# Attention scores in three steps of 512 columns, and an instruction order planned with a fuller model of TensorE

## Chip, cores, metric

One NeuronCore of one Trainium2 chip. The metric is the device time of one execution in microseconds (us), median over several executions. An execution is called *slow* when it is more than 1.5% above the fastest of the same kernel; ratios use the other, *fast*, executions alone. The 95% interval of a ratio is given in brackets.

## The reference, cut

Causal attention with a decay (8 batches, 8 heads, 576 positions, 64 columns a head), then a mixture of experts that sends each whole batch to one of 8 experts.

```python
def _attn_ref(q, k, v, f):                    # q, k, v: 8 x 8 x 576 x 64
    scores = scale * q @ k^T
    cum = np.cumsum(np.log(np.clip(f, 0.0001, 1.0)), axis=-1)
    scores = where(causal, -1e9, scores + cum[:, :, :, None] - cum[:, :, None, :])
    attn = softmax(scores)
    return attn @ v
def _moe_ref(x, w_gate, w1, w2):              # x: 8 x 576 x 512, w1: 8 x 512 x 1024, w2: 8 x 1024 x 512
    logits = x.mean(axis=1) @ w_gate          # one row a batch
    e = argmax(logits); gate = softmax(logits)[e]
    out = gate * (np.maximum(x @ w1[e], 0) @ w2[e])
```

## The kernel before

A *quad* is four heads of one batch, so there are 16. The kernel does not fix the order of its instructions by hand. It lists operations with a duration, an engine, what they wait for and which buffers they take. A small planner (class `Order`) then plays the schedule forward on the host and emits each instruction when its model of the chip would start it. The planner's times are a model; only the order reaches the chip. Each engine works its queue in order, so an instruction that waits holds up all behind it.

```python
STEPS = (((0, 0, 448, 0),),                       # (key chunk, first query, last query, column)
         ((1, 128, 576, 0),),
         ((2, 256, 576, 0), (4, 512, 576, 320)),
         ((3, 384, 576, 0), (0, 448, 576, 192)))
WIDTH = (448, 448, 384, 320)
FILL = 60.0
PM0 = 12.0
LAG = 3
...
    HOP = 0.12                                     # from one engine's end to another's start
...
            if best is None and self.filler is not None and now < self.fill_until and busy["PE"] <= now + 1e-9:
                ...self.filler(ok[0][1])           # a matmul on a zero tile, to keep TensorE busy
...
    def gate6(op, b):                              # the gate's value to all 128 partitions
        i = od.slot(("gate", b))
        nc.sync.dma_start(GATE[i], ROW[i])
...
        g6 = od.add(f"g6{b}", "SP", .5, lambda op, b=b: gate6(op, b), prio=-5, after=[g5], lands=.2, grain=.02, runs=8)
...
                raws[g, 1].behind = ... [wvs[g - LAG][0]]       # q and k of quad g, loaded behind V of quad g - LAG
...
                hm = od.add(f"H{b}{j}{half}", "PE", .49, ..., after=[ld if b else quarters[j // 2], g6], ...)
```

Note the last line: in the plan the first expert matmuls wait for `g6`. On the chip they do not use the gate; only the ReLU after them does.

The softmax here doesn't subtract the row's maximum and nothing guards it: scores larger than these inputs give would overflow.

## Time and profile before

| | before |
|---|---|
| time, median (lowest to highest) | 252.76 us (252.37 to 253.58), 3 runs |
| profiled span | 250.8 us |
| TensorE / ScalarE / GpSimd / VectorE busy | 92 / 71 / 51 / 46% |
| first gate matmul, first expert matmul | 32.5 us, 39.3 us |
| expert matmuls of the last batch, first kind: first start, last start | 228.4 us, 236.1 us |

The page's lines for the engines, the 40 slices and the chain are in the prediction below. One group is the transfer that spreads the gate. This is the view of all instructions that use the gate's tile in the kernel before: name of the group, durations of the issue, start times; the last line is for its transfers.

```profile
L567 SPq DMA_DIRECT2D gate_b<-row x8: 523/538/567, 35.5 to 216.6; - x8
...
DMA to landing us min/median/max: 2.0/6.3/17.7
```

512 bytes take up to 17.7 us to land; much else is in flight then.

### The profile page before, as it was taken

How to read it: one execution, taken by the hardware profiler on the slowest of the kernel's cores; microseconds unless marked ns; L12 is line 12 of the kernel's file. 1: busy time of each engine (PE TensorE's matmuls, PEld its weight loads, DVE VectorE, ACT ScalarE, POOL GpSimd, SP SyncE). 2: the span in 40 equal slices, each digit the busy share in tenths (PEclk: the TensorE clock that was granted, in tenths of full speed). 3: DMA queues.
4: the chain of work that ended last, by engine and by line, in shares of the span. 5: the costliest groups of instructions: out<-in, count | busy, mean ns of one | idle time of the engine just before them, and what ended most of it. 6: DMA issues, size and time to landing. Idle time of an engine off the chain costs nothing.

```text
span 250.8 us, 8039 instructions
## 1 busy us (share of the span) xinstructions
PE 229.7 (92%) x3304; PEld 146.2 (58%) x3325; DVE 115.4 (46%) x305; ACT 177.2 (71%) x313; POOL 127.0 (51%) x197
## 2 busy tenths in 40 slices
PE   6799997999889999799999999899998999999990
PEld 2333734674366846567458755586586656957840
DVE  3892882667533941278136942694146342200000
ACT  3466846897799968849779874896488787855820
POOL 6046739971995546714992649363822872300000
PEclk9657999999999999979999999999999999999996
DMA  6996849999999999990999999999993598299032
GB/s 119 221 221 118 146 73 180 201 207 212 177 220 212 215 204 226 297 213 8 173 219 213 277 218 215 254 227 209 227 278 76 82 232 216 36 212 256 29 121 75
DMA packets 59946, 45.84 MB, mean 183 GB/s; under 512 B 40896, under 2 KB 43968, under 8 KB 59904
## 3 DMA queue, kind: packets, MB, share of 16 engines
q0 software_dynamic: 14848, 26.22, 59.1%
q1 hardware_dynamic: 32576, 15.90, 25.1%
q10 hardware_dynamic: 12480, 3.15, 6.1%
q8 instruction: 28, 0.46, 0.7%
q14 instruction: 14, 0.11, 0.1%
HBM read 62.03 MB, written 9.44 MB: 285 GB/s over the span
## 4 chain that ended last, share of the span: by engine, by line
PE 73%; DMA 7%; issue 6%; POOL 6%; ACT 3%; DVE 2%; POOLq 1%; ACTq 0%; DVEq 0%
PE ps_w L595 24%; PE ps_w L612 20%; PE ps_s L400 12%; PE ps_w L439 11%; PE ps_w L615 3%; PE ps_w L680 3%; DMA out_dram<-otile 3%; DMA w1e<-in_moe_w_dram 2%; ACT e L406 2%; DMA rawq<-in_q_dram 2%; POOL e L410 2%; POOL vb L423 1%; DVE qt L387 1%; POOL rawk L281 1%; PE ps_w L548 1%
## 5 line engine op out<-in xcount | busy, mean ns | idle before, releaser
L406 ACT ACTIVATE e<-ps_s 128x896 bf16<-128x896 f32 (+2 forms) x128 | 100.2, 834 | 28.7 <-PE ps_s L400 27.9
L410 POOL TENSOR_SCALAR_AFFINE_SELECT e<-e 128x512 bf16<-128x512 bf16 x64 | 41.7, 656 | 69.0 <-ACT e L406 68.4
L595 PE MATMUL ps_w<-xT,w1e 128*128 128x288 bf16 x512 | 71.0, 292 | 3.4 <-DVE xT L459 1.9
L595 PEld LDWEIGHTS <-w1e 128*128 128x128 bf16 x512 | 60.5, 139 | 11.5 <-issue 4.9
L612 PE MATMUL ps_w<-w2e,h1T 128*128 128x512 bf16 x239 | 57.5, 380 | 1.9 <-issue 1.4
L400 PE MATMUL ps_s<-qt,kt 32*128 32x448 bf16 (+4 forms) x768 | 42.1, 289 | 5.6 <-ACT e L406 2.8
L459 DVE SCALAR_TENSOR_TENSOR xT<-ps_w,lr 128x256 bf16<-128x256 f32 (+1 forms) x64 | 26.8, 455 | 37.1 <-ACT lr L449 30.6
L605 ACT ACTIVATE h1T<-ps_w,gate_b 128x288 bf16<-128x288 f32 x77 | 37.4, 499 | 4.9 <-PE ps_w L595 4.7
L612 PEld LDWEIGHTS <-h1T 128*128 128x128 bf16 x256 | 22.8, 98 | 28.5 <-issue 3.6
L603 DVE TENSOR_SCALAR h1T<-ps_w,gate_b 128x288 bf16<-128x288 f32 x51 | 25.3, 505 | 28.6 <-PE ps_w L595 28.2
L400 PEld LDWEIGHTS <-kt 32*128 32x128 bf16 x768 | 17.6, 95 | 27.5 <-issue 21.5
L439 PE MATMUL ps_w<-e,vb 128*32 128x320 bf16 (+4 forms) x1024 | 29.4, 251 | 1.8 <-issue 1.5
L423 POOL TENSOR_TENSOR vb<-vf,WF 128x512 bf16<-128x512 f32 x29 | 30.5, 1053 | 0.3
L387 DVE STREAM_TRANSPOSE kt<-rawk 128x576 f32<-128x576 f32 (+1 forms) x17 | 21.3, 1252 | 19.4 <-DMA rawk<-in_k_dram 16.3
L624 ACT COPY otile<-ps_w 128x512 f32<-128x512 f32 (+1 forms) x25 | 14.0, 560 | 21.9 <-PE ps_w L612 20.9
L439 PEld LDWEIGHTS <-vb 128*32 128x32 bf16 x1024 | 21.3, 97 | 7.0 <-issue 4.7
L387 DVE STREAM_TRANSPOSE qt<-rawq 128x576 f32<-128x576 f32 (+1 forms) x17 | 21.1, 1244 | 0.6 <-DMA rawq<-in_q_dram 0.5
L680 PE MATMUL ps_w<-still 128*128 128x512 bf16 x51 | 17.4, 472 | 2.1 <-DVE still L313 1.4
L622 DVE COPY otile<-ps_w 128x512 f32<-128x512 f32 (+1 forms) x15 | 9.0, 599 | 21.2 <-PE ps_w L612 19.8
L439 PE MATMUL ps_w<-e,WB 128*32 128x192 bf16 (+4 forms) x512 | 17.3, 253 | 0.1
L576 POOL DMA_DIRECT2D w1e<-in_moe_w_dram x14 | 10.2, 731 | 13.1 <-DVE h1T L603 11.4
L444 ACT ACTIVATE lr<-ps_w 128x256 f32<-128x256 f32 (+1 forms) x31 | 12.7, 411 | 4.8 <-PE ps_w L439 4.5
(55 smaller groups left out, 129.4 us busy)
## 6 DMA issues: line engine op xcount, KB each, us to landing
w2e<-in_moe_w_dram POOLq DMA_DIRECT2D x8, 1024.0 KB, 14.2
out_dram<-otile SPq DMA_DIRECT2D x32, 256.0 KB, 7.4
w1e<-in_moe_w_dram POOLq DMA_DIRECT2D x14, 512.0 KB, 7.6
rawk<-in_k_dram POOLq DMA_DIRECT2D x15, 288.0 KB, 7.2
rawq<-in_q_dram POOLq DMA_DIRECT2D x15, 288.0 KB, 8.7
vf<-in_v_dram SPq DMA_DIRECT2D x12, 256.0 KB, 9.3
vf<-in_v_dram ACTq DMA_DIRECT2D x12, 256.0 KB, 12.2
vf<-in_v_dram SPq DMA_DIRECT2D x22, 128.0 KB, 6.0
```

The costliest lines, as they stand in the source:

```text
L387: nc.vector.transpose(dst, raw)
L400: nc.tensor.matmul(ps[:, col:col + i1 - i0], kt[32 * h:32 * h + 32, KLO[c]:KLO[c] + P, r], qt[32 * h:32 * h + 32, i0:i1, r], start=(r == 0 ...
L406: nc.scalar.activation(e[:, 2 * n:2 * n + 2, :], PS_S[od.slot(("s", (g, s, n)))][:, :, 0:WIDTH[s]], AF.Exp, scale=0.125)
L410: nc.gpsimd.affine_select(out=e[:, :, 0:128], in_=e[:, :, 0:128], pattern=[[0, 4], [1, 128]], channel_multiplier=-1, base=0, compare_op=AL ...
L423: eng.tensor_tensor(vb[:, c, :, :], vf[:, c, h, :], WF[:, b, c, h].unsqueeze(3).to_broadcast([P, 2, 4, D]), op=ALU.mult)
L439: nc.tensor.matmul(ps[32 * h:32 * h + 32, lo - i0:hi - i0], lhs, e[s][:, h, col:col + hi - lo], start=(n == 0), stop=(n == len(parts) - 1) ...
L459: nc.vector.scalar_tensor_tensor(XT[od.slot(("x", b))][:, mm, i0:i1], ps[:, 0:i1 - i0], 1.0 if (g, blk) in ON_DVE else LN_SCALE, LR[od.slo ...
L595: nc.tensor.matmul(ps[:, 0:288], lhs, xT[:, m, 288 * half:288 * half + 288], start=(m == 0), stop=(m == 3))
L603: nc.vector.tensor_scalar(dst, ps[:, 0:288], g[:, 0:1], 0.0, op0=ALU.mult, op1=ALU.max)
L605: nc.scalar.activation(dst, ps[:, 0:288], AF.Relu, scale=g[:, 0:1])
L612: nc.tensor.matmul(ps, h[:, j, P * sb:P * sb + P], r, start=(j == 0), stop=(j == 7))
L680: od.filler = lambda i: nc.tensor.matmul(PS_W[i], still[:, 0:P], still[:, 0:512])
```

## The change

The intent: 3 exponentials of 1024 columns a pair of heads instead of 4 narrower ones; a faster start (fillers only from 28 us, V after the small `f`); and a plan closer to the chip (cold clock, TensorE's instruction blocks of 128 matmuls, corrected durations). With it: GpSimd weights 64 more rows of V, VectorE takes part of the masks and key copies, and the gate is spread by a matmul.

```diff
-STEPS = (((0, 0, 448, 0),), ((1, 128, 576, 0),), ((2, 256, 576, 0), (4, 512, 576, 320)), ((3, 384, 576, 0), (0, 448, 576, 192)))
+STEPS = (((0, 64, 576, 0),),
+         ((1, 128, 576, 0), (None, 0, 64, 448)),
+         ((2, 256, 576, 0), (3, 384, 576, 320)))
+COLD = (1.9, 24.0)
+AHEAD = 34
+FETCH = 5.7
+STALL = 2.0
+MASKS = (2, 3)
-FILL = 60.0
+FILL = (28.0, 60.0)
-PM0 = 12.0
-LAG = 3
+PM0 = 10.0
+LAG = 2
-LOOK = {1: (0, 0, 0), 2: (0, 1, 2), 3: (1, 0, 2), 4: (1, 0, 2)}
+LOOK = {1: (0, 0, 0), 2: (0, 1, 2), 3: (1, 0, 2)}
 ... (planner)
+            if e == "PE" and now < COLD[1]:
+                op.us *= COLD[0]
+            if e == "PE":
+                wait, reached, at = self.stall(op, now)      # the fetch of the next block
+                op.us += wait
 ... (V loads)
-    last = [loadf]
+    last = []
+    mark0 = od.add("mark0", "DVE", .08, lambda op: mark(op, 0), prio=-1, after=[loadf])
 ... (gate)
-        g6 = od.add(f"g6{b}", "SP", .5, ..., lands=.2, grain=.02, runs=8)
+        g6 = od.add(f"g6{b}", "PE", .15, ..., mm=2, prio=-5, after=[g5], takes=(("bank", ("spread", b)),))
+        g7 = od.add(f"g7{b}", "DVE", .1, ...)
-                hm = ... after=[ld if b else quarters[j // 2], g6]
+                hm = ... after=[ld if b else quarters[j // 2]]
 ... (durations of some twelve kinds of operation corrected; clamping of the weights folded into the scan)
```

## The prediction

> **What bounds the kernel now.** I read the page first, then the busy time in 10 us and 1 us windows, the chain in order of time, the groups by form, and the timeline where the windows showed a hole. The page says TensorE for most of the span, and half speed near the start.
>
> ```profile
> PE 229.7 (92%) x3304; PEld 146.2 (58%) x3325; DVE 115.4 (46%) x305; ACT 177.2 (71%) x313; POOL 127.0 (51%) x197
> ...
> PE   6799997999889999799999999899998999999990
> ...
> PEclk9657999999999999979999999999999999999996
> ...
> PE 73%; DMA 7%; issue 6%; POOL 6%; ACT 3%; DVE 2%; POOLq 1%; ACTq 0%; DVEq 0%
> ```
>
> 92% busy does not mean 92% useful: matmul spans overlap, fillers on a zero tile (L680, 17.4 us) count, and at half clock everything counts double. So I counted what the matmuls are worth when the clock is full and nothing is waited for, from the stretches of the chain where one kind follows another directly:
>
> ```profile
> 130.02 0.51 PE ps_s L400 x8
> ...
> 138.62 0.40 PE ps_s L400 x16
> ...
> 228.59 7.84 PE ps_w L595 x64
> 236.43 0.99 PE ps_w L615 x16
> ...
> 237.58 6.87 PE ps_w L612 x31
> ```
>
> Per batch the first expert matmuls cost 7.84 us, the second 6.87 + 0.99. A quad (four heads; 16 of them) takes 0.51 + 0.51 + 0.45 + 0.40 = 1.87 for scores, and, from 0.61, 0.70 and 1.16 pieces of L439 in the same view, 2.47 for attention times values. Gate matmuls: about 0.28 a batch. Sum: 8 x 7.86 + 8 x 7.84 + 16 x 4.34 + 2.2 = **197 us of useful TensorE work** out of 250.8. The other 54 us lie in three places.
>
> **(a) Before 44.0 us**, when expert matmuls begin to run without holes. Up to there only 144 of 768 score, 192 of 1536 value and 20 of 512 expert matmuls ran: 3 x 1.87 + 2 x 2.47 + 2.5 = 13 us of work, **31 us lost**. The other loss here is the clock: 1 us windows show it at half from 7.8 to 21.3 us, though TensorE is called busy.
>
> ```profile
> 9.00:10.00 1.00, 1.00 (x5) 0.13 (x2) 0.97 (x2) 0.99 (x2) 0.00 (x0) 0.50 1.20 218
> ...
> 20.00:21.00 1.00, 1.00 (x7) 0.16 (x9) 0.00 (x0) 0.00 (x0) 0.94 (x4) 0.50 0.07 19
> 21.00:22.00 1.00, 1.00 (x28) 0.39 (x28) 0.00 (x0) 0.26 (x1) 0.94 (x3) 0.78 0.34 25
> ```
>
> What fills it is fillers, and they stand ahead of real work in an in-order queue:
>
> ```profile
> 12.73 1.46 PE L680 MATMUL ps_w<-still 128*128 128x512 bf16 x3
> ...
> 18.64 2.31 PE L680 MATMUL ps_w<-still 128*128 128x512 bf16 x5
> ...
> 20.88 0.82 PE L400 MATMUL ps_s<-qt,kt 32*128 32x448 bf16 x8
> ```
>
> The planner expected those scores at another time than the chip delivered them. The path then is: attention of batch 0 done, gate matmul at 32.55, expert index 33.95, weight issues on POOL from 35.5, first expert matmul 39.1, steady at 43.9.
>
> **(b) From 44 to 244.5 us**: 200.5 us holding 184 of work, **16.5 us lost**. Named holes: 67.6 to 74, where scores wait for the exponentials while POOL alone carries the chain (1.0 + 0.44 + 0.26, then 0.43 at 79); 104.5 to 110, where a transpose waiting for its load holds up the normalisations that free a PSUM bank (1.86 idle, then 12 expert matmuls in 3.00 instead of 1.47 us, because the clock fell to half again); instruction fetches in the middle of small matmuls at 159.9 and 188.8 (0.61 and 0.90). Together some 7 us; the rest are array changes and crumbs.
>
> **(c) The end**: 6.3 us from the last matmul to the landed output. From 212.6 us on there is no attention left and TensorE runs without holes, so whatever is saved earlier reaches the end.
>
> **What the Trainium skill says.** "TensorE: Matmul & The Clock Gate", Part 1, has the array at half clock until it was busy for a window of some 3.4 us, and again after an idle one. This trace agrees on the half and on the fall near 106 us, but not on the budget: 13.5 us passed here with TensorE called busy and the clock at 0.50. The same page, "Back-to-back issue gap", gives about N/2.4 + 2.5 ns: 216 ns at 512 and 122.5 at 288 columns; this trace has 216 and 122 to 123 start to start, so columns, not instruction counts, set the price. Part 3 of the page says that matmuls on different row groups run side by side; here four start within 3 to 4 ns, and a group of four costs columns/2.4 plus roughly 12 ns. "SBUF — State Buffer", on its shared port pair, says a VectorE operation with two SBUF inputs and a GpSimd one that reads SBUF shut each other out. The trace fits: weighting V on VectorE took 0.69 us alone at 13.4 us, and 1.23 each at 17.1 us beside GpSimd.
>
> **The change part by part.**
>
> *Scores.* 448/448/384/320 become 3 x 512, and the matmul count stays 48 a quad (8, 24, 16). Steps 0 and 2: 2 x (213 + 12) + 90 ns for the change of array = 0.54, and 2 x (133 + 12) + 2 x (80 + 12) + 90 = 0.56. Step 1 has 2 x (187 + 12) = 0.40 plus 16 of 64 columns whose pairs sit on one row group; the trace has such a pair 29 ns apart, so 8 pairs at about 32 = 0.26, plus 0.09: 0.75. Sum 1.85 against 1.87: **nothing, -0.3 us** over 16 quads. The saved step is eaten by the unshared 64-column pairs.
>
> *Exponentials.* Pairs took 1.73, 1.73, 1.51 and 1.30: 6.27 a quad. Slope from 913 ns at 896 and 807 at 768: 0.83 ns an element; a pair of 1024 is 1.73 + 2 x 0.107 = 1.94, times 3 = 5.83. ScalarE saves 0.44 a quad, 7 us in all, but it is idle 29%; only the first two quads have it on the path (about 0.9 us, inside the start below).
>
> *Values.* Parts go from 2 + 6 to 3 + 5, columns unchanged: 0. *Masks, copies:* POOL sheds 0.4 to 1.3 us a quad when VectorE takes two of five masks, and takes on 0.6 for another 64 rows of V and maybe 0.3 for the copied keys: about even outside quads 2 and 3.
>
> *Gate.* The spreading DMA (6.3 us median to landing, waited for nowhere in this trace) becomes a matmul and a copy: 8 x 0.15 = **+1.2 us** of TensorE, no gain seen.
>
> *Start.* No fillers before 28 us in the plan, half-speed matmuls assumed until 24, V loads held until F has landed, clamping of the weights folded into the scan and the flag postponed. Delays that go: fillers ahead of the transposes of the cumulative sum, 1.0 (scan over 9.45, transposes 10.61); ahead of the second half's first scores 1.0 (bank free near 13.1, issue 14.12); 0.8 at 15.9 to 16.7; 1.4 of the five before 20.88 (last exponential over at 19.44); 0.5 from earlier q and k. Against it, the clock may rise at 24 rather than 21.3 us: half of 2.7 us, some +0.7 to 1.4. Net **-4.0 us**, carried one for one through the gate and the weights.
>
> *Plan.* Fetches cost two holes of 1.5 us; the planner now sees them: -1.2. Masks on VectorE and corrected durations: -1.5 of the 2.1 us at 67 to 79. The bank wait with its cold clock: half of 3.4, -1.7, since nothing in the change aims at it, only truer durations. Sum **-4.4**.
>
> Total -0.3 + 1.2 - 4.0 - 4.4 = -7.5; 252.76 - 7.5 = 245.3, rounded to **245.0 us**.
>
> **Rivals.** *One: the start does not move.* Without fillers the array stays at half speed to 28 us or later, and score and value work there (some 16 us when cold) becomes the bound in place of fillers. For it: half clock lasted 13.5 us even with them. Against it: real work was waiting on fillers, not on TensorE. Then about 249. *Two: holes only move.* DMA is 91% busy by queue shares (59.1 + 25.1 + 6.1), loads of q and k queue behind 2 MB of weights, and a transpose waiting for one blocks VectorE in order, as at 105 us; masks on VectorE lengthen that queue and fight GpSimd for the port. A tighter plan meets this more often. Then -4 at the start and nothing after: 248 to 249. *Three: everything fits.* The truer model removes most of 16.5 us in (b), and batch 0 comes 6 us earlier: 239 to 240.
>
> **Range and chances.** Three parts add: -2 to -6 from the start, 0 to -8 from the plan, +0 to +2 from score pairs and gate. Their likely ends give 240.5 to 249.5. Two per cent faster is 247.7 us, 2.7 above my value with a spread of some 3.5 either way: 0.76 faster, 0.22 within, 0.02 slower (only if the cold start bites and the pairs cost twice my figure).
>
> **What would show it.** Right: the first gate matmul near 28.5 rather than 32.55 us and the first expert matmul near 35; no L680 line before some 25 us; TensorE start to start per quad still near 1.85 for scores; ScalarE's exponentials near 93 us in sum; no TensorE hole over 0.5 us by instruction fetch. Wrong: the clock at 0.50 beyond 26 us; step 1 of the scores over 0.9 us; new idle of TensorE behind VectorE or behind loads of q and k in 60 to 110 us; a chain that runs through the extra V weighting on POOL.

## The result and the profile after

The changed kernel took 256.62 us median (255.8 to 257.48, 4 runs), the kernel before in the same rounds 253.13 (252.37 to 253.58). The ratio is 1.0141, 95% interval 1.0097 to 1.0186: **slower by 1.4%**, within the 2% class, and outside the predicted range of 240.5 to 249.5. All ratios here are the mean time of one kernel's fast runs over that of the kernel before in the same rounds, so not quite the ratio of the medians. On another occasion the same changed kernel came to 1.0307 (1.0216 to 1.0399); the sign is safe, the size is not better known than 1 to 4%. The outputs are right.

The page of the changed kernel, the lines that answer to those in the prediction:

```profile
PE 222.2 (87%) x3284; PEld 145.6 (57%) x3305; DVE 147.7 (58%) x382; ACT 165.1 (65%) x264; POOL 119.3 (47%) x193
...
PE   0838989879999987799998999999999999999990
...
PEclk9999999999999999999999999999999999999998
...
PE 69%; DMA 10%; issue 5%; POOL 5%; DVE 4%; ACT 3%; POOLq 1%; ACTq 0%; DVEq 0%
```

TensorE is busy 7.5 us less, since 34 of its 51 fillers are gone (17.4 us of them before, 4.5 after); VectorE has 32 us more. The chain holds more DMA and VectorE and less TensorE than before. The 15th to 17th slice of TensorE (8, 7, 7; about 89 to 108 us) are the new thin stretch.

Nothing was won at the start: the first gate matmul is at 32.5 us in both, the first expert matmul at 38.9 against 39.3. TensorE's waits in the first 26 us of the changed kernel (what waited, for what: us in total, times, longest):

```profile
PE ps_s L481 <- DVE mid L418: 7.5, 1, 7.5
PE ps_s L481 <- DVE qt L458: 4.1, 1, 4.1
```

The scores of quad 1 wait 4.1 us for its transposed q. GpSimd issued its load only at 10.1 us, after a wait of 2.7 us for V, and the load landed at 17.3; V was itself held until `f` had landed.

TensorE's waits from 44 to 240 us, first before, then after:

```profile
PE ps_s L400 <- ACT e L406: 2.5, 5, 1.0
PE ps_w L595 <- DVE xT L459: 1.9, 1, 1.9
PE ps_w L439 <- issue: 1.5, 2, 0.9
PE ps_w L612 <- issue: 1.4, 9, 0.2
PE ps_w L595 <- DMA w1e<-in_moe_w_dram: 0.5, 1, 0.5
```

```profile
PE ps_s L481 <- ACT e L486: 1.8, 4, 0.6
PE ps_w L712 <- DVE xT L542: 1.7, 1, 1.7
PE ps_w L522 <- POOL e L382: 1.6, 2, 1.0
PE ps_w L729 <- issue: 1.4, 9, 0.2
PE ps_w L522 <- DVE xT L542: 1.4, 1, 1.4
PE ps_w L712 <- DVE h1T L720: 1.2, 2, 0.6
PE ps_w L712 <- ACT lr L527: 1.1, 1, 1.1
PE ps_w L657 <- DVE row L653: 0.5, 1, 0.5
```

The 1.5 us line of L439, which waits for nothing that the profile shows and which I read as instruction fetches, is gone, as intended. In their place stand waits for VectorE, ScalarE and GpSimd. I also counted, from the start times of single matmuls between 44 us and the last expert matmul of the first kind, where the next start came over 0.3 us later than the matmul's own columns explain (0.5 us at a change of kind): **8 holes of 8.0 us before, 14 holes of 12.4 us after**. So there are 4.4 us more of holes, against 3.5 us more of time. A recount by the same rule gave 8.8 us (13 holes) and 12.6 us (16): the small holes near the limit move the count, but hardly the difference. By stretches, most of it lies between 75 and 110 us: there TensorE is idle for 5.1 us (35 less 29.90 busy), before for 2.5 (35 less 32.48).

Two of these holes in the chain of waits of the changed kernel, in order of time (start, us, what); first the one near 54 us, where VectorE stands in order behind a load of k, with the normalisation that TensorE needs queued behind the transpose:

```profile
41.16 12.04 DMA rawk<-in_k_dram
...
53.23 0.04 DVE kt L458
...
54.33 0.50 DVE xT L542 x2
```

and the one from 96 to 106.6 us, where GpSimd alone carries the chain, with masks and weighting of V:

```profile
99.00 1.26 POOL e L382 x2
...
100.33 0.62 POOL vb L510
...
101.02 1.04 POOL vb L506
```

So the trace names suspects: the late loads, the added side work on VectorE and GpSimd (L510 is the added weighting of 64 rows), and the order. The experiments take them one at a time.

### The profile page after: what moved, and what is told of

It is laid out like the page before. It is cut to its first block, busy times and chain, and to the rows that moved or that the text cites.

```text
span 254.8 us, 7985 instructions
## 1 busy us (share of the span) xinstructions
PE 222.2 (87%) x3284; PEld 145.6 (57%) x3305; DVE 147.7 (58%) x382; ACT 165.1 (65%) x264; POOL 119.3 (47%) x193
## 4 chain that ended last, share of the span: by engine, by line
PE 69%; DMA 10%; issue 5%; POOL 5%; DVE 4%; ACT 3%; POOLq 1%; ACTq 0%; DVEq 0%
PE ps_w L712 24%; PE ps_w L729 22%; PE ps_w L522 10%; PE ps_s L481 9%; DMA rawk<-in_k_dram 5%; PE ps_w L732 3%; DMA rawq<-in_q_dram 3%; DMA vf<-in_v_dram 2%; ACT e L486 2%; DVE xT L542 1%; POOL w1e L682 1%; PE ps_w L638 1%; POOL e L382 1%; DVE lr L536 1%; POOL vb L506 1%
## 5 line engine op out<-in xcount | busy, mean ns | idle before, releaser
L486 ACT ACTIVATE e<-ps_s 128x1024 bf16<-128x1024 f32 x96 | 93.2, 1020 | 27.8 <-PE ps_s L481 22.5
L712 PEld LDWEIGHTS <-w1e 128*128 128x128 bf16 x512 | 59.8, 139 | 12.7 <-issue 7.9
L382 POOL TENSOR_SCALAR_AFFINE_SELECT e<-e 128x512 bf16<-128x512 bf16 (+2 forms) x51 | 30.0, 596 | 52.6 <-ACT e L486 52.1
L481 PE MATMUL ps_s<-qt,kt 32*128 32x512 bf16 (+3 forms) x512 | 38.7, 348 | 14.8 <-DVE mid L418 7.5
L720 DVE TENSOR_SCALAR h1T<-ps_w,gate_b 128x288 bf16<-128x288 f32 x71 | 35.7, 515 | 26.2 <-PE ps_w L712 25.2
L722 ACT ACTIVATE h1T<-ps_w,gate_b 128x288 bf16<-128x288 f32 x57 | 28.2, 499 | 18.6 <-PE ps_w L712 17.6
L542 DVE SCALAR_TENSOR_TENSOR xT<-ps_w,lr 128x256 bf16<-128x256 f32 (+1 forms) x64 | 26.6, 453 | 21.2 <-ACT lr L532 18.5
L522 PE MATMUL ps_w<-e,vb 128*32 128x320 bf16 (+3 forms) x1024 | 29.7, 259 | 1.9 <-DVE xT L542 1.4
L481 PEld LDWEIGHTS <-kt 32*128 32x128 bf16 x512 | 12.4, 96 | 30.1 <-issue 15.3
L458 DVE STREAM_TRANSPOSE kt<-rawk 128x576 f32<-128x576 f32 (+1 forms) x17 | 21.3, 1253 | 10.2 <-DMA rawk<-in_k_dram 10.1
L492 DVE TENSOR_TENSOR e<-e,causal 128x512 bf16<-128x512 bf16 (+1 forms) x32 | 17.3, 547 | 9.5 <-ACT e L486 9.4
L668 POOL DMA_DIRECT2D w1e<-in_moe_w_dram x14 | 10.1, 727 | 23.3 <-DVE row L653 11.9
L522 PE MATMUL ps_w<-e,WB 128*32 128x320 bf16 (+3 forms) x512 | 18.5, 264 | 1.8 <-POOL e L382 1.6
L522 PEld LDWEIGHTS <-WB 128*32 128x32 bf16 x512 | 11.8, 99 | 12.5 <-issue 9.8
## 6 DMA issues: line engine op xcount, KB each, us to landing
rawq<-in_q_dram POOLq DMA_DIRECT2D x15, 288.0 KB, 12.6
```

The source lines that it names most:

```text
L382: nc.gpsimd.affine_select(out=x, in_=x, pattern=[[0, x.shape[1]], [1, x.shape[2]]], channel_multiplier=-1, base=base, compare_op=ALU.is_ge ...
L458: nc.vector.transpose(dst, raw)
L481: nc.tensor.matmul(ps[:, col:col + i1 - i0], kt[row, KLO[c]:KLO[c] + P, r], qt[row, i0:i1, r], start=(r == 0), stop=(r == 1))
L486: nc.scalar.activation(e[:, lo:lo + 2, :], banks, AF.Exp, scale=0.125)
L492: nc.vector.tensor_tensor(x, x, keep.unsqueeze(1).to_broadcast([P, 4, n]), op=ALU.mult)
L522: nc.tensor.matmul(ps[32 * h:32 * h + 32, lo - i0:hi - i0], lhs, e[s][:, h, col:col + hi - lo], start=(n == 0), stop=(n == len(parts) - 1) ...
```

## The experiments

Before any run, one comparison needs no chip: with the fetch model switched off (`STALL = 0.0` and its wait set to 0) the changed kernel's instruction lists are **the same on all five engines**. The modelled instruction blocks, which gave the change its name, do not alter one instruction's place.

### First call: the start

**e1**, V loads not held for `f`:

```diff
-    last = []
+    last = [loadf]
...
-   after=[mark0] if b + c == 0 else [], behind=last if b < VQ else ...
+   behind=last if b < VQ else ...
```

> The changed kernel with the loads of V issued at once, as before the change, not held until F has landed; the order of TensorE stays the same, one mask moves from GpSimd to VectorE. Theory A (the start lost its gain because holding V held the q and k loads of the second quad behind it): the second quad's q, transposed at 17.33 us in the changed kernel, is transposed near 15, its scores begin at 16.4 instead of 18.65, the first gate matmul comes at 30.5 to 31 instead of 32.5, and the time falls by 1.5 to 2 us to about 254.8. Rival (the half-speed array or VectorE sets the start): scores of the second quad earlier, but the gate matmul within 0.5 us of 32.5 and the time the same.

**e2**, q and k of quad 4 issued right behind those of quad 3, on GpSimd's queue only:

```diff
-        nc.gpsimd.dma_start(RAW[j][od.slot(("raw", g))][32 * lo:32 * hi], src)
+        for g in (3, 4) if g == 3 else () if g == 4 else (g,):
+            ...nc.gpsimd.dma_start(RAW[j][0 if g == 4 else od.slot(("raw", g))][32 * lo:32 * hi], src)
```

> The changed kernel with the q and k loads of the fifth quad issued right behind those of the fourth, so ahead of the 2 MB of expert weights of batch 0 in the same queue; every engine's order is otherwise the same. Theory B (the middle is lost where a transpose stands at the head of VectorE's queue and waits for a load that sits behind weights): the 2.24 us wait of VectorE at 51 to 53 us and the 1.69 us hole of TensorE at 53 go, the second gate matmul comes at 53 instead of 55.6, and the time falls by 2 us to about 254.5. Rival (the loads only change places, the weights land later by as much): the first expert matmuls come 1 to 2 us later than 38.9 us and the time stays.

**e3**, nine fillers in the hole before quad 1's scores:

```diff
         i = od.slot(("qt", g))
+        if (g, s, halves) == (1, 0, (0,)): nine times od.filler(...)
```

> The changed kernel with nine fillers in the 4.1 us hole before the second quad's scores (14.2 to 18.65 us), order otherwise the same. Theory C (taking out the fillers kept the array at half speed some 7 us longer): matmuls run at full speed from about 20 us instead of 28, the value matmuls at 26 us take 1.0 instead of 2.05 us, the gate matmul comes at 31 or earlier, and the time falls by 1 to 1.5 us. Rival (ScalarE and VectorE set this stretch): full speed earlier but the gate matmul within 0.5 us of 32.5 and the time the same.

**e4**, the kernel before without its fillers of the first 20.5 planned us; the order of the real work is unchanged:

```diff
-    od.filler = lambda i: nc.tensor.matmul(PS_W[i], still[:, 0:P], still[:, 0:512])
+    od.filler = lambda i: nc.tensor.matmul(...) if max(od.clock, 0) > 20.5 else None
```

> The kernel before, without its 28 fillers of the first 26 us; the order of all real work stays. My prediction's step (fillers stood ahead of real work, some 4 us): the second quad's scores begin near 19 instead of 20.88 us, the gate matmul comes at 29 to 30 instead of 32.55, the time falls by 3 us to 250. Rival (fillers warmed the array and cost nothing on the path): half speed lasts to 26 us or later, the gate matmul comes at 33 to 34, the time grows by 1 us or more.

Measured (before 251.16 us; times of events from the traces):

| run | time | ratio (95%) | first gate | first expert | last expert block begins |
|---|---|---|---|---|---|
| changed kernel (first call of all) | 256.62 | 1.0141 (1.0097 to 1.0186) | 32.5 | 38.9 | 232.4 |
| e1 | 256.03 | 1.0228 (1.0132 to 1.0324) | 30.2 | 36.6 | 231.6 |
| e2 | 258.13 | 1.0318 (1.0197 to 1.0439) | 31.9 | 38.4 | 234.0 |
| e3 | 258.11 | 1.0297 (1.0216 to 1.0378) | 32.6 | 39.0 | 235.2 |
| kernel before | 252.76 | 1 | 32.5 | 39.3 | 228.4 |
| e4 | 252.04 | 1.009 (0.999 to 1.019) | 29.4 | 36.9 | 226.9 |

**What follows.** Holding V did cost the start: without it the gate comes 2.3 us earlier. And fillers did stand ahead of real work in the kernel before: without them its gate comes 3.1 us earlier, close to my sum. But of 2.3 us only 0.8 are left at the last batch, of 3.1 only 1.5, and neither kernel is measurably faster. **A gain at the start is not carried one for one.** For e4 the interval shows it: 3.1 us carried in full would be a ratio of 0.988, and the interval begins at 0.999. For e1 it is only suggested: its 0.8 us is less than what two traces of the unchanged changed kernel differ by (in the later trace, g4 below, the last block begins at 235.0 instead of 232.4). That waits after 44 us absorb the gain is a reading. Loading quad 4 early (e2) and filling the hole (e3) gain nothing. In e2 VectorE no longer waits for that load near 54 us, yet TensorE has one wait of 2.3 us there where it had 1.7; in e3 the 40 value matmuls near 26 us still take 2.23 us, so the fillers did not make them faster.

### Second call: the settings

**f1**: the changed kernel's operations with the old settings (fillers 0 to 60, no cold clock, no fetch model, masks on GpSimd, LAG 3, PM0 12, V at once).

> The changed kernel's operations (three steps of 512, the gate matmul, the extra rows of V) under the settings of the kernel before: fillers from 0 to 60, no doubled TensorE times before 24 us, no instruction fetches in the model, all masks and key copies on GpSimd, the lag of 3 and the start of the expert work at 12 as before, V loads at once. Theory P (the operations cost nothing, the order that the new settings made is what loses): ratio to the kernel before between 0.985 and 1.005. Theory O (the new operations cost the time: GpSimd's extra rows of V, the unshared pairs, the gate matmul): still 1.01 to 1.025.

**f2**: masks and key copies on GpSimd only.

```diff
-MASKS = (2, 3)
+MASKS = ()
-... ("DVE", "POOL") if g in MASKS or i > 2 else "POOL" ...      # also for the key copies
+... "POOL" ...
```

> The changed kernel with one part undone: all masks and key copies back on GpSimd, planned anew. If VectorE's longer queue (58% busy against 46%) is what keeps transposes and normalisations waiting near 53, 89 and 101 us, the holes of TensorE there shrink and the ratio to the kernel before falls from 1.014 (first measurement of the changed kernel) to 1.00 or lower, although GpSimd is then the fuller engine. If VectorE only waits in order for loads of q and k, moving the masks does nothing for it: 1.01 to 1.03.

**f3**: `COLD = (1.0, 0.0)`.

> The changed kernel planned without doubling TensorE's times before 24 us; fillers still only from 28 us. Its planned first gate matmul is 3.6 us earlier. If the start gain is absorbed downstream whatever its size (theory A2: waits between 44 and 110 us set the time), the gate comes at 31 to 33 us and the time stays at a ratio of 1.01 to 1.03. If the doubled times in the model are what spoils the order after 44 us, the ratio is 0.99 to 1.005.

**f4**: `HOP = 0.13`.

> The changed kernel with one constant of its model changed by 10 ns: the time from one engine's end to another's start 0.13 instead of 0.12 us. No operation differs, only the order. Theory L (the order is so sensitive that any nudge moves the time by one or two per cent): the first gate within 0.5 us of 32.5, and a time that differs from that of the changed kernel by 2 us or more in one direction or the other; the plan itself expects it 5.8 us later. If the time stays within 1 us of 256.6, the loss is in what all such orders share, that is in the operations or in the start.

Measured, before 250.65: f1 259.95, ratio 1.0256 (1.0131 to 1.0381), two of its four runs slow, its profile too; f2 257.29, 1.0255 (1.0129 to 1.038); f3 258.29, 1.0226 (1.0082 to 1.037), first gate 31.4; f4 261.84, 1.049 (1.0371 to 1.0608), first gate 31.8.

**What follows.** No setting undone by itself, and not all of them together, brings the time back. So theory P in its simple form (old settings, good order) fell. But each of these runs also got a new order (plans of 248.6 us for f1 and 249.4 for f2, against 245.8 for the changed kernel), so f2 by itself does not clear VectorE's masks; that needs a fixed order. f4 shows what a nudge can do: with no operation changed, 10 ns in the model went with about 2% more than the control of the next call (1.0307, 1.0216 to 1.0399; the intervals just overlap). Its own plan was 5.8 us longer too. That pointed to the order itself.

### Third call: suspected costs taken away at a fixed order

These three give a wrong result; the instructions stand in the same order as in the kernel that they come from.

**g1**: the side work that the change added is cut down. It was meant to become nearly free; see below for how much went.

```diff
-            nc.vector.tensor_tensor(x, x, keep...to_broadcast([P, 4, n]), op=ALU.mult)
+            nc.vector.tensor_tensor(x[:, 0:1, 0:8], x[:, 0:1, 0:8], keep[:, 0:8].unsqueeze(1), op=ALU.mult)
-            eng.tensor_tensor(vb[rows, d, :, :], vf[rows, c, h, :], ...)       # the added 64 rows
+            eng.tensor_tensor(vb[rows, d, 0:1, 0:8], ...)
-        eng.tensor_copy(kt[:, 9:12:2, :], kt[:, 0:9:8, :])
+        eng.tensor_copy(kt[:, 9:12:2, 0:4], kt[:, 0:9:8, 0:4])
```

> Wrong result on purpose. The changed kernel in exactly its order, with the side work that the change adds made nearly free: VectorE's masks touch 8 columns of one head, the extra 64 rows of V 8 columns of one head, the copied keys 4 columns of 64 (some 17 us off VectorE and 20 off GpSimd). Theory O (the added side work on VectorE and GpSimd makes the holes between 44 and 110 us): those holes go, 3 us or more faster than the changed kernel of the same call. Theory D (the loads of q and k, behind the weights, set the holes near 53 and 89 us, and the side work only rides along): less than 1.5 us.

**g2**, and **g3** as its control on the kernel before: a quarter of the second weights is loaded.

```diff
-   W2[w]...,            moe_w2[...].rearrange("o (p m) n -> p (o m n)", m=8)
+   W2[w]...[:, 0:1024], moe_w2[...].rearrange("o (p m) n -> p (o m n)", m=8)[:, 0:1024]
-            r = w2[:, j, :]
+            r = w2[:, j % 2 if b else j, :]
```

> Wrong result on purpose. The changed kernel in its order, with a quarter of the second weights loaded from the second batch on (0.25 instead of 1 MB; the matmuls read the same two slices over again). Theory D: loads of q and k land some 4 us after issue instead of 12, the holes at 53 and 89 us go, 3 us or more faster than the changed kernel. Theory O: at most 1 us.

> Wrong result on purpose, the control of the run above: the kernel before, in its order, with the same quarter of the second weights. If the transfers cost the changed kernel more than the kernel before, this one gains less than half of what the run above gains; if both gain alike, the transfers don't make the difference between the two kernels.

**g4**: the changed kernel unchanged.

> The changed kernel unchanged, as the control of this call: ratio to the kernel before 1.01 to 1.03.

Measured, before 251.1: g1 257.1, ratio 1.0191 (1.0122 to 1.026); g2 258.45, 1.0268 (1.0208 to 1.0328); g3 249.5, 0.9916 (0.9829 to 1.0002); g4 258.68, 1.0307 (1.0216 to 1.0399). Holes of the same count as above: g1 13.6 us, g2 10.7, g4 14.2.

**What follows.** g1 took away only about half of the side work: VectorE's busy time falls from 149.0 us in g4 to 139.5, GpSimd's from 119.9 to 109.8, where 17 and 20 us less were expected. A mask of 8 columns still takes VectorE 347 ns, where the masks took 580 on average. These are VectorE's masks in g4, then in g1:

```profile
L492 DVE TENSOR_TENSOR e<-e,causal 128x512 bf16<-128x512 bf16 (+1 forms) x32 | 18.4, 580 | 9.1 <-ACT e L486 9.0
L492 DVE TENSOR_TENSOR e<-e,causal 128x8 bf16<-128x8 bf16 x32 | 10.9, 347 | 6.1 <-ACT e L486 6.0
```

With that half gone g1 is 1.6 us faster than g4 by the medians and 1.2% by the ratios, and their intervals overlap. So **the side work is neither cleared nor convicted**. Three quarters of a megabyte less per batch gains the changed kernel nothing measurable, and the kernel before some 0.8% (g3, interval up to 1.0002). So **the weight traffic is not what the changed kernel loses by**. g2 shows why the named wait misled. Near 54 us the load of k now comes in time, and VectorE does not wait for it; yet TensorE stands still for at least as long as before, for something else. TensorE's waits from 40 to 60 us in g2:

```profile
PE ps_w L522 <- DVE h1T L720: 2.3, 1, 2.3
```

In the changed kernel that place showed 1.7 us behind L542. And near 89 us the load of k is late in g2 too, with no weights ahead of it: GpSimd issues it only after four weightings of V, then it takes 7.03 us. This is the chain of waits of g2:

```profile
79.66 0.99 POOL vb L506
...
80.73 0.62 POOL vb L510
...
81.42 0.98 POOL vb L506
82.41 7.03 DMA rawk<-in_k_dram
```

In the changed kernel the same load was issued at 82.56 us and landed by 88.7, so less weight traffic did not shorten it. That points to the time of issue, that is to the order, rather than to bandwidth; no run moved this issue alone.

### What the two plans were worth: a table without a run

The planner's own times, from running it on the host, can be laid beside the trace. For each batch, planned and measured time of the gate matmul and of the first expert matmul (us), and the lag of the chip behind the plan:

| | gate: plan, chip, lag | first expert: plan, chip, lag |
|---|---|---|
| before, batch 4 | 128.1, 135.7, +7.6 | 151.9, 156.4, **+4.5** |
| before, batch 5 | 158.2, 164.0, +5.8 | 177.9, 180.8, **+2.9** |
| before, batch 7 | 212.1, 214.2, +2.1 | 227.3, 228.4, +1.1 |
| after, batch 4 | 137.0, 143.0, +6.0 | 152.5, 158.4, +5.9 |
| after, batch 5 | 165.7, 171.7, +6.0 | 179.2, 185.0, +5.8 |
| after, batch 7 | 213.8, 220.2, +6.4 | 225.8, 232.4, +6.6 |

By the gate of batch 4 the chip is 6 to 8 us behind either plan. They got there differently: at the first gate (plan 27.0 before, 30.9 after) the lag is 5.6 us before and only 1.6 after, so the fuller model of the start is closer to the chip there, and the changed kernel loses its 4.4 us between batches 0 and 4. The changed plan then stays 6 us ahead of the chip (8 to 9 us in g4's trace). The plan of before loses its lead at two places, 3.1 us at the first expert matmul of batch 4 and 2.9 at that of batch 5. At these two its planner had the expert matmuls wait for the transfer that spreads the gate: it lets it land at 151.8 and 177.8 us, although the weights land at 143.0 and 170.2. (It does so at batch 2 as well, 93.4 against 89.7, where the lag shrinks by only 0.9.) In the chip's trace no wait of TensorE is put down to it. **So some 6 us of the old plan appear never to have been spent on the chip**, and the change removed them from the plan. So the plans' ends, 248.0 and 245.8, promised a gain. In these terms the last expert block is planned 1.5 us earlier, the lag there is 5.5 us larger, and it starts 4.0 us later (232.4 against 228.4); the lag is defined so that this closes, so it is no proof by itself.

This made a prediction of its own, and a way to choose orders.

### Fourth call: plans struck clean, and short ones drawn

**h1**: the kernel before, its planner told that the transfer lands at once.

```diff
-  g6 = od.add(f"g6{b}", "SP", .5, ..., after=[g5], lands=.2, grain=.02, runs=8)
+  g6 = od.add(f"g6{b}", "SP", .5, ..., after=[g5])
```

> The kernel before, with one thing told differently to its planner: the transfer that spreads the gate is taken to have landed 0.5 us after issue, so that no expert matmul waits for it in the plan (on the chip none waits for it either). The plan becomes 3.9 us shorter: 244.1 instead of 248.0. Theory L (this wait exists in the plan alone, so striking it out gains nothing on the chip): the lag of the chip behind the plan no longer shrinks between 150 and 230 us, the last batch's expert matmuls start at 223.5 + 7 = 230.5 where the kernel before has 228.4, ratio 1.00 to 1.015. If the plan's gain is a gain of the chip: 3 to 4 us faster, ratio 0.985.

For h2 to h4 I let the planner alone run with 2400 random settings for each kernel (HOP 0.095 to 0.16, PM0 9 to 15, LAG 2 or 3, the priority of quad 0's values 3 to 5, the price of an array change 0 to 1) and took orders with the shortest plans. 160 draws over the same ranges, with the changed kernel, gave plans from 245.3 to 258.8 us, median 250.7. The changed kernel's own plan of 245.8 is among the best tenth of these, so the planner saw nothing wrong with it.

```diff
 h2, changed kernel, V at once        h3, kernel before, as h1 and e4      h4, changed kernel, V at once
 HOP 0.12 -> 0.0958                   HOP 0.12 -> 0.1204                   HOP 0.12 -> 0.1313
 PM0 10.0 -> 12.1                     PM0 12.0 -> 10.4                     PM0 10.0 -> 10.3
 SWITCH 0 -> 0.08                     SWITCH 0 -> 0                        SWITCH 0 -> 0.47
 PP0 4 -> 5; LOOK as before           (rest as before)                     LOOK as before
```

> The operations of the changed kernel (V loads at once as in e1) in an order drawn from 2400 settings of the planner by the shortest plan: 240.2 against 245.8. Theory L: the lag stays near 6 us, the last expert matmuls start at 220.3 + 6 = 226, so about 6 us faster than the changed kernel, ratio to the kernel before 0.98 to 1.00. Theory O: the operations lose whatever the order, ratio 1.01 to 1.03.

> The operations of the kernel before with the gate's wait struck out of the plan, no fillers before 20.5 us as in e4, and an order drawn in the same way from 2400 settings: plan 241.1. Theory L: last expert matmuls at 220.4 + 7 = 227.5, 1 us earlier than before, ratio 0.985 to 1.00, and level with h2. Theory O: faster than h2 by 4 us or more.

> A second draw with the operations of the changed kernel, plan 241.9: theory L 221.9 + 6 = 228 for the last expert matmuls, some 4 us faster than the changed kernel, ratio 0.985 to 1.005; theory O 1.01 to 1.03. Two draws, so that one lucky order does not decide.

Measured, before 250.38:

| run | plan | time | ratio (95%) | holes after 44 us |
|---|---|---|---|---|
| h1 | 244.1 | 253.38 | 1.0087 (1.0023 to 1.0152) | (profile slow) |
| h2 | 240.2 | 250.9 | 0.9997 (0.9936 to 1.0058) | 5.7 us |
| h3 | 241.1 | **246.83** | **0.9829** (0.977 to 0.9888) | 5.9 us |
| h4 | 241.9 | 250.66 | 0.9999 (0.9927 to 1.0071) | 4.4 us |

TensorE's waits from 44 to 240 us in h3:

```profile
PE ps_s L400 <- ACT e L406: 2.6, 6, 1.0
PE ps_w L595 <- DMA w1e<-in_moe_w_dram: 0.7, 1, 0.7
PE ps_w L615 <- issue: 0.3, 1, 0.3
PE ps_s L400 <- DVE qt L387: 0.3, 1, 0.3
```

**What follows.** h1 is the cleanest case: its plan is 3.9 us *shorter* and the chip is 0.9% *slower*. Striking out a wait that the chip did not show gained nothing. But the order changed too, and it is one order. h2 and h4 have the changed kernel's operations and run level with the kernel before, where the change's own order is 1.4 to 3% behind; their holes are 5.7 and 4.4 us instead of 12.4 to 14.2. So **the order is a part of the loss**: the same operations lose 1.4 to 3% in one order and nothing in another. (They also load V at once, as e1 does, which by itself showed no clear gain.) But h2 and h4 are orders picked from many, and that of the kernel before is not. The like-for-like comparison is h3, the old operations in an order picked in the same way. It is the fastest kernel, 4 us faster than h2 (4.1) and h4 (3.8) at a like plan, where theory L had wanted it level and theory O "faster than h2 by 4 us or more". So **the operations cost about 1.7% in picked orders**, as much as the change's whole loss at its first measurement (1.4%), and a better order was worth 1.7% to the old operations too. Which part is the larger is not settled: these are two picked orders against one. One sign says where the 4 us lie: the holes of the three are about equal, yet from the first gate to the last expert block h3 takes 193.3 us (29.8 to 223.1), h2 196.5 (31.5 to 228.0) and h4 196.1 (30.2 to 226.3). So about 3 us look like work in TensorE's queue rather than waiting.

### Fifth call: the rest

**i1**: h4 at the same order, the gate spread by the old transfer; matmul and copy are left out.

```diff
-        nc.tensor.matmul(ps[:, 0:1], ROW[i], one)
+        nc.sync.dma_start(GATE[i], ROW[i])
...
-        nc.vector.tensor_copy(GATE[i], ps[:, 0:1])
+        pass
```

> The kernel of h4 in the same order, with the gate spread by the transfer of the kernel before instead of the matmul and its copy. If the gate matmul makes the rest of 4 us (it stands in TensorE's queue ahead of work that could run, and waits for a chain over ScalarE and VectorE), ratio to the kernel before 0.980 to 0.990. If it costs only its own time, some 0.3 us a batch: 0.990 to 0.997, as 8 x 0.3 = 2.4 us at most. If nothing: 1.000 as h4.

**i2**: the three-step scores with the gate's transfer and with masks on GpSimd, in a drawn order (HOP 0.1121, PM0 12.7, SWITCH 0.80, plan 241.3).

> The three-step scores and the rest of the changed kernel, but with the gate's transfer in place of the matmul, all masks and key copies on GpSimd, V loads at once, in an order drawn from 3000 settings with a plan of 241.3. If the score steps themselves cost nothing, level with h3: ratio 0.978 to 0.990. If they and the work they bring make the rest of 4 us: 0.995 to 1.005.

Measured, before 250.86: i1 248.34, ratio 0.9878 (0.9788 to 0.9967); i2 253.56, 1.0128 (1.0026 to 1.023).

**What follows.** i1 lies 1.2% below h4, some 3 us, inside the first expectation (0.980 to 0.990), but its interval also covers most of the second, and the intervals of i1 and h4 overlap (h4's begins at 0.9927). Its trace can't help: it is of the slowest of its four executions (250.43 us), and its last expert block begins at 226.5 us, h4's at 226.3. The profile has a value for the matmul itself, the group of L657 in the changed kernel:

```profile
L657 PE MATMUL ps_w<-one,row 1*128 1x1 f32 x16 | 3.0, 256 | 0.5 <-DVE row L653 0.5
```

One call is two matmuls on the array, and in the chain of waits a pair takes 0.31 us: 8 x 0.31 = 2.5 us, plus 0.5 us of waiting. That fits i1. i2 settles nothing about the scores: its trace names a reason of its own, second weights that come late, for which TensorE waits from 50 to 53 us. TensorE's waits in i2:

```profile
PE ps_w L730 <- DMA w2e<-in_moe_w_dram: 3.3, 1, 3.3
```

Its chip is 7.5 us behind its plan at the last batch, where h4 is 4.4, h3 2.7 and h2 7.7 behind. So a short plan is no warrant: i2 has one too, and it is slower than the kernel before.

## Why the prediction was wrong, point by point

- **Scores, -0.3: too small a gain.** In the traces a group of four matmuls takes 240 ns at 512 columns, 211 at 448, 142 at 320, 85 to 89 at 192, 58 at 128, 29 at 64. Summed without array changes that is about 1.5 us a quad in both kernels. I had charged 0.26 us for the 16 matmuls of 64 columns, taking 29 ns for a pair; it is the time of four, and the 16 take 0.12. Step 1 so costs 0.63 us with its array change, not 0.75. In the way the prediction counts, from the chain, a quad takes 0.56 + 0.63 + 0.56 = 1.75 us against 1.87: some -1.9 us over 16 quads.

```profile
67.48 0.56 PE ps_s L481 x8
...
70.36 0.51 PE ps_s L481 x8
70.87 0.12 PE ps_s L479 x16
...
73.60 0.56 PE ps_s L481 x16
```

- **Exponentials, 5.83 us a quad: right.** 93.2 us in all for 96 of 1020 ns; 16 x 5.83 = 93.3.
- **Values, 0: right.** Groups of four by width are equal in both kernels (136 ns at 320, 82 at 192, 57 at 128, 28 at 64).
- **Gate, +1.2: too small by half.** It is 2.5 us of TensorE by the profile; i1 gives 3 with a wide interval.
- **Fetches, -1.2: the holes went** (1.5 us of L439 before, none after), but not through the model of the fetches, which moves no instruction. That the new order happens to have none is luck, as far as these runs show.
- **Start, -4.0 "carried one for one through the gate and the weights": wrong twice.** The gate came at 32.5 us as before: 0 instead of -4.0. V held for `f` delayed quad 1's q and k, and that is some 2 us of it (e1 has the gate at 30.2 us, the two traces of the changed kernel at 32.5 and 31.9); the rest stays open. The sum itself gives -3.3 to -4.0, and I had taken its far end. And where the start did come earlier, it was not carried: e4's 3.1 us at the gate are 1.5 at the last batch and no gain in time.
- **Plan, "-4.4": wrong, and this is the step that decides.** I assumed that truer durations would close the holes that I had named and open no others. The new order has 4.4 us *more* holes (8.0 before, 12.4 after), with new waits for VectorE, ScalarE and GpSimd. The 1.5 us for masks and the 1.7 for the bank wait came back as other waits. That the planner itself saw a gain (248.0 to 245.8) comes from a wait that only the old plan had.
- **What I left out: the operations.** I had them at -0.3 + 1.2 + 0 = +0.9 us. In picked orders they cost about 4 us (h3 against h2 and h4): 2.5 of it is the gate matmul, and the rest is not placed.
- **Rival Two was the nearest.** (Its DMA shares add up to 90.3%, or 91.1 with the two instruction queues.) "Holes only move" is what happened, and my list of what would show me wrong named idle of TensorE behind VectorE and behind loads of q and k in 60 to 110 us, and a chain through the extra weighting of V. All of these appeared; the clock at 0.50 and a step 1 over 0.9 us did not. But of its *mechanism*, the loads behind 2 MB of weights are not the main cause (g2: a quarter of the second weights gains nothing), while VectorE's longer queue stays open, since g1 removed only half of the work. Its 248 to 249 also still had the start's gain in it.

Shown: no start gain arrives at the gate of the changed kernel, and e4's is not carried; the order matters by 1.4 to 3% at the same operations (h2, h4 against the changed kernel); in picked orders the operations cost about 1.7% (h3 against h2, h4); less weight traffic gains nothing (g2). Suggested: the old plan's wait is not real (the lag table, h1); 2.5 to 3 us for the gate matmul (the profile, i1). Open: whether order or operations are the larger part of the loss; how much of it is the added side work on VectorE and GpSimd, which g1 only halved; the rest of 1 to 2 us between i1 and h3 (intervals overlap); and how fast the three-step scores would be in a good order, as i2 failed for another reason.

## What to carry to other kernels

A planner's end time may be compared between two versions only after each plan has been laid beside a trace: where the lag shrinks at one operation, look there for a wait that the plan has and the chip does not. A list schedule can jump by several us on a nudge of 10 ns (f4: a plan 5.8 us longer), so judge a change of the operations over several drawn orders on both sides, not one, and draw orders before changing operations: here that was worth 1.7% to the old operations, while the change lost 1.4 to 3%. And the wait that a trace names last is only the last: take it away at a fixed order before you believe it, since another of equal length may stand behind it, and read in the trace how much you really took away.

## What the Trainium skill lacked or had wrong

- "TensorE: Matmul & The Clock Gate", Part 1, gives a few microseconds (about 3.4) of warm-up. In the kernel before, the clock stayed at 0.50 for 13.5 us of busy time. In the changed kernel, the record of the clock says 1.00 from 8 us on, but 40 value matmuls of 320 columns took 2.05 us at 26.2 us and about 1.22 at 82.8 (the second line is from the chain, which ends a piece where the next begins). So the record can miss a slow stretch. The same part of the page warns that such clock events have been seen to be unreliable. This trace agrees; go by the durations:

```profile
26.23 2.05 PE L522 MATMUL ps_w<-e,vb 128*32 128x320 bf16 x40
```

```profile
82.76 1.22 PE ps_w L522 x40
```

- "Runtime: NRT & Kernel Launch", Instruction fetch mechanics, says that engines fetch blocks of 16 KiB and that the cost is mostly hidden. The block size agrees (28 packets, 0.46 MB in all, in both kernels: 16.4 KB each). If the holes of 0.61 and 0.90 us among short matmuls in the kernel before are fetches, it was not hidden there. The trace speaks for it without proving it: packets of the instruction queue start at 158.2 and 187.6 us, just before the holes at 159.9 and 188.8.
- "DMA: Bandwidth & Descriptors", Latency and other measured facts, has a fixed cost of some 2 us. The 512-byte transfer of the gate landed after 2.0 us at best, but after 6.3 in the median and 17.7 at most beside other traffic. I found no page with a figure for so small a transfer in such traffic.
- No page has the sensitivity of an in-order schedule to its order: 10 ns in a model constant went with some 2% of the time (1.049 against 1.031 for the same operations; the intervals just overlap).
